# Feature group 1 of the last two token chunks by seven products, between groups 9 and 10; a weight split and a PSUM sum moved

## The chip, the cores and the metric

The kernel runs on one core of a Trainium2 chip. The metric is the device time of the program in microseconds (us), as the median of several runs. Engines are named as in the profile: PE (TensorE matmul), PEld (TensorE weight load), DVE (VectorE), ACT (ScalarE), POOL (GpSimd), SP (SyncE, which here only issues DMA transfers). L12 is line 12 of the kernel before. Differences of under about 0.2% of the time are not told from no change.

## The reference

One layer: a layer norm, a windowed dilated attention (S = 2048 tokens, D = 640, 32 heads of 20, 8 keys at a distance of 2), a bilinear feed-forward part with F = 1536 features, and a gate.

```python
xn = layernorm(x)
q, k, v = split_heads(xn @ wqkv)              # 32 heads of 20
idx = pos[:, None] - 2 * arange(8)            # 8 keys, dilation 2, masked below 0
attn = softmax(where(mask, q . k[idx] * scale, -1e9))
s = (attn . v[idx]) @ wo
h = (xn @ w_gate) * (xn @ w_up)               # 2048 x 1536
return x + s * silu(h @ w_down)
```

All is fp32.

## The kernel before, in words

*Products.* TensorE works on fp32r operands. Each fp32 operand is split into a high part (a copy by ACT, L114) and a low part (the difference, by POOL in L115 or by DVE), and a product is the sum of three: high by high, high by low, low by high (`ALL3`, L117; in `mm3` and in `group` the low part of the weights comes in the last third of the matmuls).

*Tiling of gate and up.* The tokens lie in four chunks of 512, the features in twelve groups f of 128 columns of gate and 128 of up. `gate_up(f, ch)` does group f for one chunk directly: 15 matmuls of 128x512 for gate, 15 for up (L124). `group(f, c0, second)` (L1253) does a pair of chunks (c0 and c0 + 1) and gate and up together by a seven-product scheme (Strassen's, in Winograd's form): 54 matmuls (L1292) in the order j = 0, 5, 2, 1, 4, 3, 6 into three PSUM banks, "g", "q" and "u". Between products ACT copies a bank to SBUF (`hold`, L1261, after the first, third, fourth and fifth product), DVE adds (`gate_b` L1264, `gate_a` L1274) and multiplies (`up_a` L1277), and `up_b` (L1267) and `h_b` (L1270) run on DVE for chunks 2 and 3, on POOL for chunks 0 and 1. A finished part of h goes to memory by SP (`store_h`, L1250). A bank is free for the next product when its hold is done.

*The weights of a group.* `load_wf(f)` brings the raw weights (640 KB, SP, L180). POOL makes five sums of their parts (S1, S2, S3, d5, S4; `w_add`, L1238), and they are split in four pieces by `w_split`: G (the tile "pk", read by the group's first product) and S, R, U (tiles "s"). Each split is an ACT copy, then a POOL difference. There are two "wraw" buffers for raw weights and for sums, so a load also waits until POOL has read the raw weights before it. The table `two_places` says after which product of which half of the group before each step is issued: the load after the first product of the first half, the sums from there to the second product of the second half, the splits in the second half.

*Order of the program.* Groups 0 and 1 are done early by `gate_up` on all four chunks, between the layer norm and the products of q, k and v (`qkv`). Groups 2 to 10 follow, each as two half-groups: chunks 2 and 3 (`group(f, 2)`), then chunks 0 and 1 (`group(f, 0, 1)`). Group 11 and the product with w_down come last. In the early part POOL also makes the sums of the tokens of chunks 0 and 1 that the seven products need (`early_sums`), and `early_high(k)` (L616, L617) makes their high and low parts, which SP stores for group 2 and later. `split_wq(1)` splits the weights of the next q, k, v products, on POOL for the low parts.

*The attention* is a generator that `advance(budget)` moves on by a sum of costs: products and reductions on DVE (L542, L549, L508), additions on POOL (L514), stores of the result by SP (L590). Each half-group gives it 54 x 0.184 units, each `qkv` after the start 1.9, each half (gate or up) of a `gate_up` there 3.25. What is left of it is flushed in group 10.

*The last loop* runs over products m of h with w_down (L866): `sum_h` (L813 and on) and `lo_h` (L829) on DVE prepare later products, `gather(m)` reads out PSUM on DVE (L882, L886, L889) or ACT, which frees the bank.

Every engine and every DMA queue works through its own list in the order of issue and waits on semaphores, so an instruction that waits holds up all behind it on its engine.

Of the kernel before, what the change touches and what calls it, by code (L numbers as in the profile page):

```python
# [12 lines left out]
F32R = mybir.dt.float32r  # L13
# [6 lines left out]
P = 128  # L20
# [9 lines left out]
TPC = CH // P  # L30
# [12 lines left out]
NP = NT // 2  # L43
PAIRS = range(0, W, 2)
PACE = 1.0
VEC = 2
EARLY = 1
GROUP_RATE = 0.184

# [7 lines left out]
def kernel(  # L57
# [70 lines left out]
    def slot(shape, dt=F32R):  # L128
        return st(shape, "s", SLOTS, dt)
# [48 lines left out]
    def load_wf(f):  # L178
        wf_raw[f] = slot([P, KD, 2, P], F32) if f == 0 else st([P, KD, 2, P], "wraw", 2)
        nc.sync.dma_start(wf_raw[f], wgu[f])  # L180
# [430 lines left out]
    def early_high(k):  # L611

        r0, r1, a, b = early_t[:4]
        for n, (j, y) in enumerate((("T1", a), ("T2", b), ("T3", r0), ("T4", r1))):
            hi = early_t[4 + n].bitcast(F32R)
            nc.gpsimd.tensor_copy(hi, y)  # L616
# [497 lines left out]
    gate_up(0, 2)  # L1114
    trans_q(15)
    low_parts()
    early_high(1)
    for a in range(2):
        nc.sync.dma_start(e_scr[2 + a], xT[3][a][:, 0:2, :].bitcast(F32))
    made.add(0)  # L1120
# [1 line left out]
    for i in range(TPC, NE):  # L1122
        qkv(0, 1, i)
        advance(PACE * 1.9)
    split_wq(1, nc.gpsimd)
    gate_up(1, 2)
    gate_up(0, 3)
    gate_up(1, 3)

    f0, f1 = KF - 2, KF - 1  # L1130
    F_TWO = 2
    tt, tw, steps = {0: [], 2: []}, {}, []
    T_UNIT = {(j, a, k): divmod(n, 3) for n, (j, a, k) in
              enumerate((j, a, k) for k in range(2) for j in ("T1", "T2", "T3") for a in range(2))}
# [66 lines left out]
    w_sum = {}  # L1201

    def two(f):
        return F_TWO <= f < f1

    def w_unit(f, name, k=0):

        t, n = W_UNIT[name]
        if t == "U" and two(f):
            t, n = "R", n + 1  # L1210
        if t not in tw:
            tw[t] = st([P, 2, KD, P], "pk", 1, F32R) if t == "G" and f >= F_TWO else slot([P, 2, W_ROWS[t], P])
        return [tw[t][:, i, n + k] for i in range(2)]

    def w_split(f, *names):
# [13 lines left out]
    def w_add(f, *names):  # L1229

        if f not in w_sum:
            w_sum[f] = st([P, 9, P], "wraw", 2)
        r, t = wf_raw[f], w_sum[f]
        v = {"A11": r[:, 0:2, 0], "A12": r[:, 2:4, 0], "A21": r[:, 0:2, 1], "A22": r[:, 2:4, 1], "g5": r[:, 4, 0],
             "u5": r[:, 4, 1], "S1": t[:, 0:2], "S2": t[:, 2:4], "S3": t[:, 4:6], "S4": t[:, 6:8], "d5": t[:, 8]}
        for name in names:
            a, b = W_SUM[name]
            nc.gpsimd.tensor_tensor(v[name], v[a], v[b], op=ALU.add if name == "S1" else ALU.subtract)  # L1238
# [14 lines left out]
    def group(f, c0=0, second=0):  # L1253

        b = {"A": pt([P, CH], "g", 2), "C": pt([P, CH], "u", 2), "B": q_one}
        kept, later = {}, []
        eng = nc.vector if c0 and f >= VEC else nc.gpsimd

        def hold(j):
            kept[j] = st([P, CH], "gh", 5)  # L1260
            nc.scalar.activation(kept[j], b["ACACABA"[j]], AF.Copy)  # L1261

        def gate_b():
            nc.vector.tensor_add(kept[2], kept[2], b["C"])  # L1264

        def up_b():
            eng.tensor_add(kept[1], kept[1], kept[4])  # L1267

        def h_b():
            eng.tensor_mul(kept[2], kept[2], kept[1])  # L1270
            store_h(f, c0 + 1, kept[2])

        def gate_a():
            nc.vector.tensor_add(kept[0], kept[0], b["B"])  # L1274

        def up_a():
            nc.vector.tensor_mul(kept[0], kept[0], b["A"])  # L1277
            store_h(f, c0, kept[0])

        if not second:  # L1280
            if not two(f - 1):
                w_split(f, "U")
            w_sum.pop(f, None)
            wf_raw.pop(f)
        for n, j in enumerate((0, 5, 2, 1, 4, 3, 6)):
            y = b["ACACABA"[j]]
            runs = [(w_unit(f, H_IN[j], k)[i], x_in(W_IN[j], l, k, c0)) for i, l in ALL3 for k in range(2)]
            if j in FIVE:
                name, ch = FIVE[j]
                runs += [(w_unit(f, name)[i], xT[c0 + ch][l][:, KD - 1, :]) for i, l in ALL3]  # L1290
            for r, (w, x) in enumerate(runs):
                nc.tensor.matmul(y, w, x, start=j in (0, 1, 5) and r == 0, stop=r == len(runs) - 1,  # L1292
                                 skip_group_check=True)
            if j in (0, 1, 2, 4):
                hold(j)
            finish_piece()
            if (second, n) == (1, 6) and (second, n) in places:
                places.pop((second, n))(f)
            for act in later:
                act()  # L1300
            later = {5: [gate_a], 3: [gate_b, up_b]}.get(j, [])
            if j == 6:
                unfinished.extend([up_a, h_b])
            if (second, n) in places:
                places[second, n](f)
            if (f, second, n) in beside:
                beside[f, second, n]()
            if (second, n) == (0, 0) and f < f1 and f + 1 not in wf_raw:
                load_wf(f + 1)
            advance(PACE * len(runs) * (GROUP_RATE if two(f) else 0.184))  # L1310

    places = {}
# [89 lines left out]

    wo_keep = []
    def sums(*names):
        return lambda f: w_add(f + 1, *names)

    def splits(*names):
        return lambda f: w_split(f + 1, *names)

    two_places = {(0, 5): sums("S1"), (0, 6): sums("S2"), (1, 0): sums("S3"), (1, 1): sums("d5", "S4"),  # L1410
                  (1, 2): splits("G"), (1, 4): splits("S"), (1, 5): splits("R"), (1, 6): splits("U")}
# [8 lines left out]
            load_e(1, 0, 0)  # L1420
            load_e(1, 1, 1)

    for f in range(2, f1):
        places.clear()
        places.update(two_places)
        if f == F_TWO:
            for n in range(3):
                places[0, n] = lambda f, n=n: load_late(n)
        group(f, 2)
        group(f, 0, 1)  # L1430
    places.clear()
    beside.update({(f1, 0, 0): lambda: split_wo(1, nc.vector),
                   (f1, 0, 2): lambda: (turn_pair(0), load_pair(1)), (f1, 0, 4): lambda: (hi_pair(0, 0), lo_pair(0, 0)),
# [193 lines left out]
```

## Time and profile before

| | us |
|---|---|
| median of three runs | 738.06 (738.04 to 738.15) |
| the profiled execution, own time | 737.74 |
| its span, first to last instruction | 735.7 |
| PE busy | 729.2 |
| DVE busy | 629.1 |
| POOL busy | 449.4 |
| ACT busy | 301.0 |
| mean granted clock of TensorE | 0.999 |

A row of a timeline gives start, duration (both in us), engine, line, operation, output and inputs, the tile's shape and the count of instructions in it; in square brackets stands how long the engine had idled before it and what ended that. A duration of several instructions is that of the whole stretch. An SPq row is SP issuing a transfer, not the transfer. In the chain of work that ended last, each piece has start, duration, and engine and line.

### The profile page before, as it was taken

How to read it: one execution, taken by the hardware profiler on the slowest of the kernel's cores; microseconds unless marked ns; L12 is line 12 of the kernel's file. 1: busy time of each engine (PE TensorE's matmuls, PEld its weight loads, DVE VectorE, ACT ScalarE, POOL GpSimd, SP SyncE). 2: the span in 40 equal slices, each digit the busy share in tenths (PEclk: the TensorE clock that was granted, in tenths of full speed). 3: DMA queues.
4: the chain of work that ended last, by engine and by line, in shares of the span. 5: the costliest groups of instructions: out<-in, count | busy, mean ns of one | idle time of the engine just before them, and what ended most of it. 6: DMA issues, size and time to landing. Idle time of an engine off the chain costs nothing.

```text
span 735.7 us, 11056 instructions
## 1 busy us (share of the span) xinstructions
PE 729.2 (99%) x4030; PEld 666.0 (91%) x4030; DVE 629.1 (86%) x729; ACT 301.0 (41%) x561; POOL 449.4 (61%) x383
## 2 busy tenths in 40 slices
PE   9999999999999999999999999999999999999997
PEld 7989989988999998888888887888999999999997
DVE  7676998799796989899989999978899897777775
ACT  5668312323232333233323332334556664444442
POOL 6159919997778889797889969667644630000000
PEclk9999999999999999999999999999999999999999
DMA  8464589889766659461733542277768955555534
GB/s 325 169 204 164 214 291 302 245 257 257 183 192 174 217 194 349 123 198 58 220 92 96 180 143 73 64 229 192 215 201 244 313 221 193 193 193 194 194 108 143
DMA packets 106436, 143.78 MB, mean 195 GB/s; under 512 B 23080, under 2 KB 75556, under 8 KB 106382
## 3 DMA queue, kind: packets, MB, share of 16 engines
q1 hardware_dynamic: 88654, 121.13, 51.8%
q10 hardware_dynamic: 16000, 12.78, 5.4%
q0 software_dynamic: 1728, 9.18, 5.2%
q8 instruction: 31, 0.51, 0.3%
q14 instruction: 23, 0.19, 0.1%
HBM read 94.40 MB, written 55.67 MB: 204 GB/s over the span
## 4 chain that ended last, share of the span: by engine, by line
PE 94%; DVE 3%; issue 1%; POOL 1%; DMA 1%; SPq 0%; ACT 0%; POOLq 0%; DVEq 0%
PE g L1292 15%; PE q L434 11%; PE u L1292 10%; PE u L434 8%; PE g L434 8%; PE q L866 8%; PE u L866 5%; PE q L1292 5%; PE g L124 5%; PE u L124 5%; PE q L996 3%; PE e L866 3%; PE g L866 3%; PE u L996 2%; PE e L996 2%; PE e L434 1%
## 5 line engine op out<-in xcount | busy, mean ns | idle before, releaser
L514 POOL TENSOR_TENSOR o<-o,t 128x960 f32<-128x960 f32 (+1 forms) x66 | 132.8, 2012 | 9.4 <-DVE t L508 8.5
L508 DVE TENSOR_TENSOR t<-e,kv 128x960 f32<-128x960 f32 (+1 forms) x96 | 99.6, 1038 | 16.2 <-POOL o L514 16.2
L542 DVE TENSOR_TENSOR t<-q,kv 128x1920 f32<-128x1920 f32 (+1 forms) x48 | 92.5, 1927 | 3.2 <-DMA kv<-qkv_scr 3.1
L549 DVE TENSOR_REDUCE lg<-t 128x96 f32<-128x1920 f32 (+1 forms) x48 | 92.3, 1924 | 0.2
L434 PE MATMUL q<-s,xc 128*128 128x360 f32 (+1 forms) x450 | 82.9, 334 | 0.1
L1261 ACT ACTIVATE gh<-g 128x512 f32<-128x512 f32 x57 | 34.1, 598 | 112.8 <-PE g L1292 108.0
L115 POOL TENSOR_TENSOR s<-wraw,s 128x384 fp32r<-128x384 f32 (+6 forms) x57 | 68.4, 1214 | 17.9 <-ACT s L114 17.8
L434 PEld LDWEIGHTS q<-s,xc 128*128 128x128 f32 x450 | 74.9, 188 | 4.2 <-ACT xc L314 0.3
L434 PE MATMUL u<-s,xc 128*128 128x360 f32 (+1 forms) x360 | 65.8, 334 | 0.0
L434 PEld LDWEIGHTS u<-s,xc 128*128 128x128 f32 x360 | 60.3, 188 | 2.2
L434 PE MATMUL g<-s,xc 128*128 128x360 f32 (+1 forms) x330 | 61.5, 338 | 0.0
L434 PEld LDWEIGHTS g<-s,xc 128*128 128x128 f32 x330 | 55.7, 188 | 2.6
L1292 PE MATMUL g<-s,s 128*128 128x512 f32 x228 | 58.0, 390 | 0.0
L1292 PE MATMUL u<-xc,s 128*128 128x512 f32 x228 | 57.9, 389 | 0.0
L866 PE MATMUL q<-xc,s 128*128 128x320 f32 x342 | 55.6, 310 | 0.6 <-DVE s L886 0.6
L866 PEld LDWEIGHTS q<-xc,s 128*128 128x128 f32 x342 | 51.5, 188 | 0.8 <-ACT s L847 0.8
L1292 PEld LDWEIGHTS g<-s,s 128*128 128x128 f32 x228 | 42.7, 188 | 9.2 <-ACT gh L1261 0.4
L1292 PEld LDWEIGHTS u<-xc,s 128*128 128x128 f32 x228 | 42.8, 188 | 8.9
L114 ACT ACTIVATE s<-wraw 128x384 fp32r<-128x384 f32 (+6 forms) x58 | 32.6, 581 | 30.3 <-PE g L1292 10.2
L1292 PE MATMUL g<-xc,s 128*128 128x512 f32 x171 | 42.0, 390 | 0.3 <-ACT gh L1261 0.3
L1292 PE MATMUL q<-xc,pk 128*128 128x512 f32 x171 | 41.9, 389 | 0.0
L514 POOL TENSOR_TENSOR o<-t 128x960 f32<-128x960 f32 (+1 forms) x11 | 22.2, 2014 | 28.3 <-DVE t L508 24.9
(332 smaller groups left out, 1561.3 us busy)
## 6 DMA issues: line engine op xcount, KB each, us to landing
h_scr<-gh SPq DMA_DIRECT2D x48, 256.0 KB, 2.6
wraw<-in_wgu SPq DMA_DIRECT2D x11, 640.0 KB, 4.5
kv<-qkv_scr SPq DMA_DIRECT2D x14, 480.0 KB, 5.9
t<-h_scr SPq DMA_DIRECT2D x8, 768.0 KB, 6.2
qkv_scr<-s ACTq DMA_DIRECT2D x17, 360.0 KB, 3.9
kv<-qkv_scr SPq DMA_DIRECT2D x14, 367.5 KB, 6.8
s_scr<-gh SPq DMA_DIRECT2D x16, 320.0 KB, 3.8
gh<-s_scr SPq DMA_DIRECT2D x16, 320.0 KB, 3.9
```

The costliest lines, as they stand in the source:

```text
L114: nc.scalar.activation(hi, raw, AF.Copy)
L115: eng.tensor_sub(lo, raw, hi.bitcast(F32))
L124: nc.tensor.matmul(acc, a, b, start=first and n == 0, stop=last and n == len(runs) - 1)
L434: nc.tensor.matmul(p, xT[(r * NE + i) // TPC][a][:, k, t0:t0 + P], wq[m][b][k], start=n == 0, stop=n == len(runs) - 1, skip_group_check=ac ...
L508: nc.vector.tensor_mul(t.rearrange("p (n d) -> p n d", d=DH), e[:, :, w].unsqueeze(2).to_broadcast([P, NE * nh, DH]), v)
L514: return NE * c * cost, lambda: eng.tensor_add(y, z, t)
L542: nc.vector.tensor_mul(t, q, k)
L549: nc.vector.tensor_reduce(out=lg[:, :, j:j + 2].rearrange("p n a -> p a n"), in_=t.rearrange("p a (n d) -> p a n d", d=DH), op=ALU.add, ax ...
L866: nc.tensor.matmul(p, y[:, i, k], wd_part(name, k, l), start=new and r == 0, stop=r == len(runs) - 1, skip_group_check=True)
L996: nc.tensor.matmul(b, y, w, start=new and r == 0, stop=r == len(runs) - 1, skip_group_check=True)
L1261: nc.scalar.activation(kept[j], b["ACACABA"[j]], AF.Copy)
L1292: nc.tensor.matmul(y, w, x, start=j in (0, 1, 5) and r == 0, stop=r == len(runs) - 1, skip_group_check=True)
```

## The change

1. `gate_up(1, 2)` and `gate_up(1, 3)` go. Group 1 of chunks 2 and 3 is done by `group(1, 2)`, between groups 9 and 10. Its weights are loaded a second time. The half-group that follows for every other f, on chunks 0 and 1, isn't there, as these are done early. All that prepares group 10's weights is therefore issued in this one half-group (`one_places`): the load after the first product, the five sums after the third, the splits G, S, R and U after the fourth to the seventh.
2. `split_wq(1)` comes after the second of the four `qkv` products that follow the attention's start, instead of after the last, and `early_high(1)`, which stood ahead of them, comes directly behind it.
3. In the last loop, the step at m = 3 no longer issues `sum_h(8)` and `lo_h(7)`; they are issued at m = 4, behind that step's read-out of PSUM.

```diff
-    early_high(1)
...
     for i in range(TPC, NE):
         qkv(0, 1, i)
         advance(PACE * 1.9)
-    split_wq(1, nc.gpsimd)
-    gate_up(1, 2)
+        if i == TPC + 1:
+            split_wq(1, nc.gpsimd)
+            early_high(1)
     gate_up(0, 3)
-    gate_up(1, 3)
+    wf_raw.clear()
...
-    F_TWO = 2
+    ORDER_F = [2, 3, 4, 5, 6, 7, 8, 9, 1, f0, f1]
+    after_f = dict(zip(ORDER_F, ORDER_F[1:]))
...
             finish_piece()
-            if (second, n) == (1, 6) and (second, n) in places:
+            if n == 6 and (second, n) in places and (second or f == 1):
                 places.pop((second, n))(f)
...
-            if (second, n) == (0, 0) and f < f1 and f + 1 not in wf_raw:
-                load_wf(f + 1)
+            if (second, n) == (0, 0) and f < f1 and after_f[f] not in wf_raw:
+                load_wf(after_f[f])
             advance(PACE * len(runs) * (GROUP_RATE if two(f) else 0.184))
...
     two_places = {(0, 5): sums("S1"), (0, 6): sums("S2"), (1, 0): sums("S3"), (1, 1): sums("d5", "S4"),
                   (1, 2): splits("G"), (1, 4): splits("S"), (1, 5): splits("R"), (1, 6): splits("U")}
...
-    for f in range(2, f1):
+    one_places = {(0, 2): sums("S1", "S2", "S3", "d5", "S4"), (0, 3): splits("G"), (0, 4): splits("S"),
+                  (0, 5): splits("R"), (0, 6): splits("U")}
+    for f in ORDER_F[:-1]:
         places.clear()
-        places.update(two_places)
+        places.update(two_places if f > 1 else one_places)
...
         group(f, 2)
-        group(f, 0, 1)
+        if f > 1:
+            group(f, 0, 1)
...
+        elif m == 4:
+            sum_h(m + AHEAD)
+            lo_h(m + AHEAD - 1)
...
         after()
+        if m == 3:
+            continue
```

The other lines of the diff only bring `two`, `w_unit`, `sums` and `splits` in line with the new order of groups. In the rows below, line numbers of the changed kernel are lower by one for the code ahead of the group function.

POOL's list around the start of group 9 in the kernel before: the end of group 8 (three splits, L1267 and L1270 of its chunks 0 and 1, additions of the attention, L514), then the sums for group 10, behind its load into wraw_3979:

```order
L115 TENSOR_TENSOR s_2460<-wraw_3857,s_2460 128x768
L115 TENSOR_TENSOR s_2645<-wraw_3857,s_2645 128x384
L115 TENSOR_TENSOR s_2645<-wraw_3801,s_2645 128x384
L1267 TENSOR_TENSOR gh_3923<-gh_3923,gh_3933 128x512
L514 TENSOR_TENSOR o_3771<-o_3771,t_942 128x960
L1270 TENSOR_TENSOR gh_3909<-gh_3909,gh_3923 128x512
L514 TENSOR_TENSOR o_3771<-o_3771,t_942 128x960 x2
L1238 TENSOR_TENSOR wraw_4032<-wraw_3979 128x256
```

POOL's list around the start of group 1 in the changed kernel: the end of group 9, then the five sums and the splits for group 10, behind its load into wraw_4074:

```order
L114 TENSOR_TENSOR s_2546<-wraw_3893,s_2546 128x384
L1267 TENSOR_TENSOR gh_4013<-gh_4013,gh_4023 128x512
L513 TENSOR_TENSOR o_3790<-o_3790,t_926 128x960
L1270 TENSOR_TENSOR gh_3999<-gh_3999,gh_4013 128x512
L1238 TENSOR_TENSOR wraw_4099<-wraw_4074 128x256
L1238 TENSOR_TENSOR wraw_4099<-wraw_4099,wraw_4074 128x256
L1238 TENSOR_TENSOR wraw_4099<-wraw_4074 128x256
L1238 TENSOR_TENSOR wraw_4099<-wraw_4074 128x128
L1238 TENSOR_TENSOR wraw_4099<-wraw_4074,wraw_4099 128x256
L114 TENSOR_TENSOR pk_2497<-wraw_4074,pk_2497 128x640
L114 TENSOR_TENSOR s_2362<-wraw_4099,s_2362 128x768
```

The sums and the split of pk now stand in the half-group that also has the load. On SP, the load stands directly behind the two stores of group 9's h for chunks 0 and 1, as in before (the second of them stores what L1270 makes).

ACT's list in group 1 of the changed kernel, with its holds (L1261; gh_4125 is the fourth) and the high parts of group 10's weights (L113):

```order
L1261 ACTIVATE gh_4068<-g_4060 128x512
L570 ACTIVATE e_70<-lg_3813 128x384
L1261 ACTIVATE gh_4096<-g_4060 128x512
L1261 ACTIVATE gh_4115<-u_4061 128x512
L113 ACTIVATE pk_2497<-wraw_4074 128x640
L1261 ACTIVATE gh_4125<-g_4060 128x512
L113 ACTIVATE s_2362<-wraw_4099 128x768
```

In before the copy of pk stands between the second and the third hold of the half-group on chunks 0 and 1; here it stands between the third and the fourth of the half-group on chunks 2 and 3.

DVE's list in the last loop, at m = 3 and 4, before:

```order
L882 TENSOR_TENSOR s_5442<-u_5360,gh_5405 128x320
L813 TENSOR_TENSOR s_5447<-s_5330,wraw_5334 128x768
L829 TENSOR_TENSOR s_5444<-wraw_5328,s_5444 128x768
L886 TENSOR_TENSOR s_5468<-lg_5379,q_1_68 128x320
L815 TENSOR_TENSOR s_5447<-s_5447,wraw_5328 128x768
```

and changed:

```order
L881 TENSOR_TENSOR s_5455<-u_5373,gh_5418 128x320
L885 TENSOR_TENSOR s_5478<-lg_5392,q_1_68 128x320
L812 TENSOR_TENSOR s_5480<-s_5343,wraw_5347 128x768
L828 TENSOR_TENSOR s_5457<-wraw_5341,s_5457 128x768
L814 TENSOR_TENSOR s_5480<-s_5480,wraw_5341 128x768
```

The sum that reads PSUM (L886, now L885) has moved ahead of the two operations on h.

More of the change, by code (lines that the diff above doesn't have):

```diff
@@ L45 @@
 PACE = 1.0
-VEC = 2
 EARLY = 1
@@ L1203, in two @@
     def two(f):
-        return F_TWO <= f < f1
+        return f < f1
     def w_unit(f, name, k=0):
@@ L1211, in w_unit @@
         if t not in tw:
-            tw[t] = st([P, 2, KD, P], "pk", 1, F32R) if t == "G" and f >= F_TWO else slot([P, 2, W_ROWS[t], P])
+            tw[t] = st([P, 2, KD, P], "pk", 1, F32R) if t == "G" else slot([P, 2, W_ROWS[t], P])
         return [tw[t][:, i, n + k] for i in range(2)]
@@ L1256, in group @@
         kept, later = {}, []
-        eng = nc.vector if c0 and f >= VEC else nc.gpsimd
+        eng = nc.vector if c0 else nc.gpsimd
         def hold(j):
@@ L1280, in group @@
         if not second:
-            if not two(f - 1):
+            if f == ORDER_F[0]:
                 w_split(f, "U")
@@ L1404, in sums @@
     def sums(*names):
-        return lambda f: w_add(f + 1, *names)
+        return lambda f: w_add(after_f[f], *names)
     def splits(*names):
-        return lambda f: w_split(f + 1, *names)
+        return lambda f: w_split(after_f[f], *names)
     two_places = {(0, 5): sums("S1"), (0, 6): sums("S2"), (1, 0): sums("S3"), (1, 1): sums("d5", "S4"),
@@ L1421, in load_late @@
             load_e(1, 1, 1)
-    for f in range(2, f1):
+    one_places = {(0, 2): sums("S1", "S2", "S3", "d5", "S4"), (0, 3): splits("G"), (0, 4): splits("S"),
+                  (0, 5): splits("R"), (0, 6): splits("U")}
+    for f in ORDER_F[:-1]:
         places.clear()
-        places.update(two_places)
-        if f == F_TWO:
+        places.update(two_places if f > 1 else one_places)
+        if f == ORDER_F[0]:
             for n in range(3):
```

## The prediction

> **What bounds the kernel now.** I read the page's first lines, then the waits of TensorE, then the chain in order of time around the places that the diff touches.
>
> ```profile
> span 735.7 us, 11056 instructions
> PE 729.2 (99%) x4030; PEld 666.0 (91%) x4030; DVE 629.1 (86%) x729; ACT 301.0 (41%) x561; POOL 449.4 (61%) x383
> DVE  7676998799796989899989999978899897777775
> ```
>
> TensorE is busy for 99% of the span, so the time is the number of matmuls times their pitch plus the few waits. These are all the waits of TensorE (who waited, for whom, sum in us, times, longest):
>
> ```profile
> PE q L229 <- POOL lg masks.py:199: 1.4, 1, 1.4
> PE q L866 <- DVE s L886: 0.6, 1, 0.6
> PE g L1292 <- ACT gh L1261: 0.3, 1, 0.3
> ```
>
> A change can therefore save matmuls, remove up to 0.9 us of late waits, or make new waits. The profiled execution took 737.74 us, the median of the runs 738.06: I make the sum against 737.74 and add 0.3 at the end.
>
> **Part 1, the matmuls: -1.36 us.** The chain in order of time has group 1 of chunk 2 (from 84.76) and of chunk 3 (from 98.36) in pieces of 15 matmuls; a later half-group by seven products follows, as busy time of PE, PEld, DVE, ACT, POOL, then granted clock, DMA share and GB/s of a window:
>
> ```profile
> 84.76 3.40 PE g L124 x15
> 98.36 3.40 PE g L124 x15
> 101.76 3.40 PE u L124 x15
> 456.65:468.90 12.25, 12.25 (x56) 10.14 (x55) 12.11 (x12) 4.32 (x8) 9.80 (x9) 1.00 0.42 121
> ```
>
> 15 matmuls in 3.40 us are 0.2267 us each, so the 60 removed are 13.60 us. The 54 of the new half-group are 54 x 0.2267 = 12.24 us (the window of 456.65 spans just that). All of it lies on TensorE's path: 12.24 - 13.60 = -1.36 us.
>
> **Part 1, what the new half-group has to carry: +5.8 us.** Every other feature group has two half-groups, 24.5 us, in which the next group's weights are loaded, summed on POOL and split into high and low parts; `two_places` begins the sums in the first half and the splits only in the second. Group 1 has one half-group of 12.24 us, and `one_places` puts it all there. Call its start T. Before has a near twin: the first half of group 9 (T = 443.84), ahead of which POOL has the same list as in the new order: splits of the weights with the attention's additions between, then L1267, an addition, L1270, with the next load on SP behind the store of what L1270 made. POOL's and SP's rows there (start, us; SPq is a queue's issuing time):
>
> ```profile
> 445.26 3.81 POOL L115 TENSOR_TENSOR s<-wraw,s 128x768 fp32r<-128x768 f32 x3
> 449.04 1.29 POOL L1267 TENSOR_TENSOR gh<-gh,gh 128x512 f32<-128x512 f32 x1
> 450.30 2.25 POOL L514 TENSOR_TENSOR o<-o,t 128x960 f32<-128x960 f32 x1
> 452.51 1.28 POOL L1270 TENSOR_TENSOR gh<-gh,gh 128x512 f32<-128x512 f32 x1
> 454.27 0.46 SPq L180 DMA_DIRECT2D wraw<-in_wgu  x1
> 458.52 0.97 POOL L1238 TENSOR_TENSOR wraw<-wraw 128x256 f32<-128x256 f32 x1 [0.17 <-DMA wraw<-in_wgu]
> 459.57 0.74 POOL L1238 TENSOR_TENSOR wraw<-wraw,wraw 128x256 f32<-128x256 f32 x1
> 460.27 1.69 POOL L1238 TENSOR_TENSOR wraw<-wraw 128x256 f32<-128x256 f32 x2
> 461.92 0.74 POOL L1238 TENSOR_TENSOR wraw<-wraw,wraw 128x256 f32<-128x256 f32 x1
> 462.92 1.57 POOL L115 TENSOR_TENSOR pk<-wraw,pk 128x640 fp32r<-128x640 f32 x1 [0.26 <-ACT pk L114]
> ```
>
> *The load.* Here it is issued at T+10.43 and the weights are there at 458.52, T+14.7. In the other rows of that load, the earliest that stands at a group's start is the one of 276.89 below, in the group that began at 272.20: T+4.69, with no L1270 to wait for. The load for group 11 lands at 482.14 in the group that began at 468.90, T+13.2:
>
> ```profile
> 272.20 1.52 PE L1292 MATMUL g<-xc,pk 128*128 128x512 f32 x6
> 276.89 0.35 SPq L180 DMA_DIRECT2D wraw<-in_wgu  x1
> DMA to landing us min/median/max: 4.1/4.6/11.8
> 482.14 0.73 POOL L1238 TENSOR_TENSOR wraw<-wraw 128x256 f32<-128x256 f32 x1 [7.45 <-DMA wraw<-in_wgu]
> 484.44 2.16 POOL L1238 TENSOR_TENSOR wraw<-wraw 128x256 f32<-128x256 f32 x2
> 487.40 1.57 POOL L115 TENSOR_TENSOR pk<-wraw,pk 128x640 fp32r<-128x640 f32 x1
> ```
>
> Were POOL done at T with all but the last of the three splits (1.3), L1267, the addition and L1270, then 1.3 + 1.29 + 2.25 + 1.28 would bring L1270's end to T+6.1; ACT's copy ahead of that split and SP's issuing, 0.8 together, make it T+6.9. With 4.1 to land, the short end for this order is T+11.0; the long end is the twin's T+14.7. I take the landing L = T+13.0, nearer to the twin, because POOL's list is the twin's, less a little because the attention, from which the additions come, is spaced wider ahead of it.
>
> *First wait.* ACT has the high part of the first product's weights ahead of the fourth hold (L1261) of group 1:
>
> ```profile
> 453.83 0.60 ACT L1261 ACTIVATE gh<-g 128x512 f32<-128x512 f32 x1 [2.30 <-POOL gh L1270]
> 461.61 0.60 ACT L1261 ACTIVATE gh<-g 128x512 f32<-128x512 f32 x1 [2.80 <-PE g L1292]
> 462.11 0.73 ACT L114 ACTIVATE pk<-wraw 128x640 fp32r<-128x640 f32 x1
> ```
>
> In before that split stands in a second half, with its data long there. In the new order it waits for the landing, and the hold, 0.60, waits behind it; the seventh product needs the bank that this hold empties. It is due at T + 45 x 0.2267 = T+10.2 and starts at L + 0.73 + 0.60 = T+14.3: 4.1 us.
>
> *Second wait.* POOL's five sums and the low part of those weights took from 458.52 to 464.49 after the landing, 5.97 us. Group 10's fifth matmul reads that low part. It is due at T + 12.24 + 4 x 0.2267 = T+13.15, or T+17.3 behind the first wait; the low part is there at T+18.97: 1.7 us more. Both together are 5.97 + 13.0 - 13.15 = 5.8 us. The next low parts need POOL some 1.9 us each against 3.4 us of matmuls until they are read, so the chain ends there. POOL's row of 487.40 ends 6.8 us after its landing, with DVE at work beside it, 0.9 more: the ends of this term are 11.0 + 5.3 - 13.15 = 3.1 (five sums of 0.74 and the split of 1.57) and 14.7 + 6.8 - 13.15 = 8.4.
>
> *Other costs of part 1.* Group 1's weights are loaded a second time, 640 KB, during group 9, in whose second half DMA is 0.42 busy (window above): 0. The attention loses four early steps and gains those of the new half-group: 13.0 units of its budget against 54 x 0.184 = 9.9, so 3.1 more are left for the flush in group 10. They fall on DVE, whose tenths fall from 9 to 7 in the last quarter: 0, and 2 us at most if TensorE's holds there come to wait for it. The wait of 0.3 us on L1261 is the twin's, at 453.83; in the new order the wait above stands at that place instead: -0.3.
>
> **Part 2, the split of q, k, v ahead of the early low parts: 0.** POOL's split runs here while the removed matmuls did:
>
> ```profile
> 81.42 0.62 POOL L616 CAST kv<-kv 128x512 fp32r<-128x512 f32 x1
> 89.17 4.39 POOL L115 TENSOR_TENSOR s<-wraw,s 128x1080 fp32r<-128x1080 f32 x3
> ```
>
> It ended at 93.56 (89.17 + 4.39), and the next products of q, k, v began at 105.16. Without the 13.60 us they come at 91.56. Put ahead of the early low parts (L616 and L617, POOL's instructions from 81.42 to 89.17 here), the split starts near 81.4 and ends near 86, 5 us in time. Behind the old order it would have been 2 us late: the cost if the cover is gone. The early parts and their stores come some 4 us later, and with them, on SP, a load for the attention's next unit; TensorE waits for neither there: 0.
>
> **Part 3, the PSUM sum ahead of h's: -0.6.** DVE's rows, and the matmul that waits:
>
> ```profile
> 596.66 1.23 DVE L813 TENSOR_TENSOR s<-s,wraw 128x768 f32<-128x768 f32 x1
> 597.81 0.94 DVE L829 TENSOR_TENSOR s<-wraw,s 128x768 fp32r<-128x768 f32 x1
> 598.68 0.47 DVE L886 TENSOR_TENSOR s<-lg,q 128x320 f32<-128x320 f32 x1
> 599.30 0.97 PE L866 MATMUL q<-xc,s 128*128 128x320 f32 x5 [0.57 <-DVE s L886]
> ```
>
> L886 goes ahead of 1.23 + 0.94 us of sums, and the wait of 0.6 goes. The two sums come 0.5 us later, for a product later still: 0, and 0.5 if that has no slack.
>
> **Sum.** 737.74 - 1.36 + 5.8 - 0.3 - 0.6 = 741.3, and 0.3 for the median: 741.6 us.
>
> **A rule on the clock.** TensorE's granted clock in the first 3 us, where it worked 1.65 of 3 us after a wait of 1.4:
>
> ```profile
> 0.00:3.00 3.00, 1.65 (x3) 1.04 (x4) 0.06 (x1) 1.28 (x1) 2.33 (x11) 1.00 0.36 107
> ```
>
> It is 1.00 at once, and I charge no slowing to the new wait of 4.1 us; no gap of before is that long, so none tests it. The Trainium skill, "TensorE: Matmul & The Clock Gate", section "Part 1: The HAM clock gate", says that after an idle window of about 3.4 us the array runs at half clock until it has been busy for about as long; the row of the first 3 us doesn't agree. The rule's result is rival C.
>
> **Rivals.**
> A. *The load is early, faster.* If POOL were a whole addition or two ahead of the twin and the load were issued by T+2.8 (landing T+7.2), all waits would vanish: 738.06 - 2.3 = 735.8. What decides is the time at which POOL ends L1270. For it: the load at 276.89. Against: that one waits for no L1270, and even with its T+4.69 the low part comes 0.9 us late (4.69 + 4.1 + 5.3 - 13.15), 736.7. Chance 0.06.
> B. *The short end.* L = T+11.0 with undisturbed sums: 738.06 - 2.26 + 3.1 = 738.9, no difference that counts. For it: the two halves ahead hold less attention. Chance 0.13.
> C. *The clock falls during the first wait.* The 13 matmuls between the two waits then take up to 5.9 us instead of 2.95: from T+14.3 to T+20.2, past the low part at T+19.0, so 1.2 more, 742.8. Against: 1.00 in the first 3 us. Chance 0.06. The page's rule is this mechanism.
> D. *DVE runs later than in the twin.* Its window of group 9's second half is 12.11 us busy of 12.25, and the additions on POOL wait for it; a further addition of 2.25 ahead of L1270 gives L = T+15.3 and slower sums: 741.6 + 2.3 + 0.9 = 744.8. Chance 0.11.
>
> **How the numbers follow.** The forecast, a landing between T+11.6 and T+14.7, has 0.64. About 0.2% (1.5 us, 736.6 to 739.5) is what a measurement of this kernel can tell from no change. Slower: forecast, C and D, 0.81; same: B, 0.13; faster: A, 0.06. The range 739.0 to 744.2 takes in the long end of the wait with disturbed sums (741.6 + 2.6) and on the other side the edge of B; it leaves out A, half of B and most of D.
>
> **What would show it.** In the profile of the changed kernel: TensorE's waits name ACT gh L1261 with some 4 us and POOL's split of pk with some 2, both in the half-group between 9 and 10; the load ahead of group 10 is issued about T+8.5 behind the store of the last h; the wait on L886 is gone; L1292 has 54 matmuls more and L124 60 fewer; nothing waits for the q, k, v splits near 91. I am wrong if the load is issued before T+5, if the raw weights of group 10 are there when ACT comes to them, or if DVE's flush in group 10 becomes a new wait.

## The result, and the profile after

The changed kernel took 747.64 us (median of six executions, 745.96 to 756.11) against 738.05 us before: a ratio of 1.0151 with a 95% interval of 1.0103 to 1.0199, 9.6 us slower. The forecast was 741.6 us, with a range up to 744.2. The sign was right, and the wait that was to carry it stands where it was put; the size was not.

The profiled execution was the longest of the six, 756.11 us. First its head and the waits of TensorE:

```profile
span 754.1 us, 11079 instructions
PE g L1292 <- ACT gh L1261: 4.8, 1, 4.8
PE u L1292 <- POOL s L114: 2.2, 1, 2.2
PE q L433 <- ACT s L447: 2.1, 2, 1.5
PE g L1292 <- DMA s<-t_scr: 1.9, 1, 1.9
```

The first row is the forecast one. The wait on the PSUM sum (L886 before, L885 now) is gone. The other three rows are in the products of q, k, v and at the entrance of group 2, where I had forecast nothing. A second profile of the same kernel, an execution of 749.03 us, is nearer to the median (`again`, first of the runs below; its wait of 1.4 us at the start of the program, as before, is left out):

```profile
PE g L1292 <- ACT gh L1261: 4.7, 1, 4.7
PE q L433 <- ACT s L447: 1.4, 1, 1.4
PE g L1292 <- DMA s<-t_scr: 0.6, 1, 0.6
```

*The half-group between 9 and 10* began at T = 467.50 in the profile of 756.11 us. POOL, SP's queue, ACT and TensorE, and then TensorE's clock in the window behind the wait (busy time of PE, PEld, DVE, ACT, POOL, then granted clock, DMA share, GB/s):

```profile
473.58 1.29 POOL L1270 TENSOR_TENSOR gh<-gh,gh 128x512 f32<-128x512 f32 x1
476.33 0.88 SPq L179 DMA_DIRECT2D wraw<-in_wgu  x1
481.40 0.74 ACT L113 ACTIVATE pk<-wraw 128x640 fp32r<-128x640 f32 x1 [6.22 <-DMA wraw<-in_wgu]
482.04 0.58 ACT L1261 ACTIVATE gh<-g 128x512 f32<-128x512 f32 x1
482.67 4.21 PE L1292 MATMUL g<-xc,s 128*128 128x512 f32 x9 [4.81 <-ACT gh L1261]
485.17 1.56 POOL L114 TENSOR_TENSOR pk<-wraw,pk 128x640 fp32r<-128x640 f32 x1
482.70:488.20 5.50, 5.50 (x13) 4.34 (x14) 2.10 (x3) 1.89 (x3) 5.50 (x6) 0.50 0.00 0
```

L1270 ends at T+7.4, the load is issued at T+8.8 behind the stores of h and lands at T+13.9; ACT's split and the hold follow, and the seventh product starts at T+15.2. Then the granted clock is 0.50, and 13 matmuls take 5.50 us, 0.42 each, where they take 2.95 at full clock. POOL's low part is ready at 486.73, T+19.2, but at half clock TensorE reaches it only later, so the second wait of the sum is not seen: the slow matmuls cover it.

*The products of q, k, v.* Two rows of TensorE in the kernel before; then TensorE, SP's queue and ACT in the second profile of the changed kernel:

```profile
105.00 2.56 PE L434 MATMUL q<-s,xc 128*128 128x360 f32 x15
107.40 2.56 PE L434 MATMUL g<-s,xc 128*128 128x360 f32 x15
103.67 2.56 PE L433 MATMUL u<-s,xc 128*128 128x360 f32 x15
107.63 2.74 PE L433 MATMUL q<-s,xc 128*128 128x360 f32 x15 [1.40 <-ACT s L447]
110.21 2.63 PE L433 MATMUL g<-s,xc 128*128 128x360 f32 x15
112.68 2.63 PE L433 MATMUL u<-s,xc 128*128 128x360 f32 x15
99.61 0.97 SPq L147 DMA_DIRECT2D wraw<-in_wqkv  x2
106.62 0.60 ACT L113 ACTIVATE s<-wraw 128x480 fp32r<-128x480 f32 x1 [4.12 <-DMA wraw<-in_wqkv]
```

ACT stands from 102.5 to 106.6 at the split (L113) of weights that are still in flight, and the copy L447 that frees a bank for TensorE waits behind it. And there is a second cost that no wait shows: fifteen matmuls take 112.68 - 110.21 = 2.47 us behind the wait, 164.4 ns each in the mean of the stretch, where those ahead of it, as those at the same place in the kernel before, take 2.40 us, 160.0 ns. In this profile some 680 matmuls of 360 columns go at the slower pitch; 57 of them, ahead of 46 us, do so in before too. The others, between 108 and 263 us, cost some 625 x 4.4 ns = 2.8 us.

*The last loop.* DVE in the second profile: the sum that reads PSUM (L885) goes ahead, as the change says.

```profile
608.42 0.47 DVE L885 TENSOR_TENSOR s<-lg,q 128x320 f32<-128x320 f32 x1
608.81 0.94 DVE L812 TENSOR_TENSOR s<-s,wraw 128x768 f32<-128x768 f32 x1
```

The second profile against before, 749.03 - 737.74 = 11.3 us: matmuls -1.4, old waits gone -0.9, the wait near 106 1.4, the slower pitch 2.8, the wait for token sums 0.6, the wait in group 1 4.7, half clock behind it 2.6. That is 9.8; the rest, 1.5 us, is in gaps under 0.5 us, such as the restart behind each wait and 0.4 us behind the last matmul.

### The profile page after: what moved, and what is told of

Its sections match the earlier page's. It is cut to its first block, busy times and chain, and to the rows that moved or that the text cites. A ratio compares the mean times of both kernels' runs of the same rounds, so it can differ in the third digit from the quotient of the medians.

```text
span 754.1 us, 11079 instructions
## 1 busy us (share of the span) xinstructions
PE 736.2 (98%) x4024; PEld 670.5 (89%) x4024; DVE 626.5 (83%) x731; ACT 304.9 (40%) x568; POOL 456.0 (60%) x392
## 5 line engine op out<-in xcount | busy, mean ns | idle before, releaser
L1261 ACT ACTIVATE gh<-g 128x512 f32<-128x512 f32 x60 | 36.0, 599 | 122.0 <-PE g L1292 116.1
L114 POOL TENSOR_TENSOR s<-wraw,s 128x384 fp32r<-128x384 f32 (+6 forms) x60 | 71.1, 1201 | 20.4 <-ACT s L113 20.4
L1292 PE MATMUL u<-xc,s 128*128 128x512 f32 x240 | 61.3, 390 | 2.2 <-POOL s L114 2.2
L1292 PE MATMUL g<-s,s 128*128 128x512 f32 x240 | 61.5, 391 | 1.9 <-DMA s<-t_scr 1.9
L1292 PEld LDWEIGHTS u<-xc,s 128*128 128x128 f32 x240 | 45.3, 189 | 12.1 <-POOL s L114 2.7
L1292 PEld LDWEIGHTS g<-s,s 128*128 128x128 f32 x240 | 45.0, 188 | 11.6 <-DMA s<-t_scr 2.3
L1292 PE MATMUL g<-xc,s 128*128 128x512 f32 x180 | 46.1, 402 | 4.8 <-ACT gh L1261 4.8
L113 ACT ACTIVATE s<-wraw 128x384 fp32r<-128x384 f32 (+6 forms) x61 | 34.6, 584 | 37.4 <-PE g L1292 9.7
L1292 PEld LDWEIGHTS g<-xc,s 128*128 128x128 f32 x180 | 34.9, 195 | 12.6 <-ACT gh L1261 5.2
L1292 PE MATMUL q<-xc,pk 128*128 128x512 f32 x180 | 44.1, 389 | 0.0
```

Source lines behind the costliest of these rows:

```text
L113: nc.scalar.activation(hi, raw, AF.Copy)
L114: eng.tensor_sub(lo, raw, hi.bitcast(F32))
```

## The experiments

Theory 1: three losses that add up, the late weights of group 10 (with the half clock), the early transfers that the 60 matmuls had covered, and the slower pitch that their wait starts. Rivals stand at each run. All ratios are to the kernel before, run beside it.

**again**: the changed kernel as it is.

> The changed kernel once more, for a second profile. Theory 1 (three losses that add up): the same waits stand at the same places: about 1.5 us near 106 for ACT's copy behind a split that waits for weights, 2 to 4 us at group 2's entrance (272 and 284) for POOL's low parts and a load of token sums, 4.8 us at the fourth hold of group 1, with half clock behind the long ones. Theory 2 (only the wait in group 1 is always there, the waits at 106 to 284 belong to the one profiled execution, which took 756.1 us where the others took 746 to 750): the profile shows the 4.8 us and little else, and its time is near 747.

Measured: 750.88 us (749.03 to 754.38), ratio 1.0174 (1.0148 to 1.0201). Its profile is shown above. The wait near 106, the pitch and the 4.7 us are in both profiles; the 2.2 us on POOL and the waits of 0.3 and 0.6 near 239 and 247 are in the longer one alone. So theory 1 holds for the first three, and the longer execution has something on top (last part of this section).

**load_first**: group 10's raw weights go on SP's queue ahead of group 9's last stores.

```diff
+        if f == 9:
+            places[1, 6] = lambda f: (w_split(1, "U"), load_wf(f0))
```

> The changed kernel, with group 10's raw weights loaded ahead of the two stores of group 9's h on SP instead of behind them. Theory 1: the load is issued about T+3 (when POOL has made the last low part from the raw buffer it takes over), lands about T+8, ACT's split is done before the fourth hold is due at T+10.2, POOL's low part is ready about T+13, when it is due; the wait of 4.8 us and the half clock behind it (2.6 us) go, so 6.5 to 7.6 us faster than the changed kernel, 740 to 741. Rival (POOL's sums, not the load, set the end): the first wait goes but a second of 3 to 4 us takes its place at group 10's fifth matmul, 744.

Measured: 742.82 us (740.95 to 744.25), ratio 1.0058 (1.0040 to 1.0076). Group 1 begins at T = 460.87 here:

```profile
462.54 0.35 SPq L179 DMA_DIRECT2D wraw<-in_wgu  x1
468.17 0.73 POOL L1238 TENSOR_TENSOR wraw<-wraw 128x256 f32<-128x256 f32 x1
468.44 0.73 ACT L113 ACTIVATE pk<-wraw 128x640 fp32r<-128x640 f32 x1
469.29 0.60 ACT L1261 ACTIVATE gh<-g 128x512 f32<-128x512 f32 x1
471.07 2.20 PE L1292 MATMUL g<-xc,s 128*128 128x512 f32 x9
471.49 2.50 POOL L114 TENSOR_TENSOR pk<-wraw,pk 128x640 fp32r<-128x640 f32 x1
```

The load leaves at T+1.7, ACT finds the weights there, the seventh product starts at its due time and the low part is ready at T+13.1, when it is due at T+13.15. Neither the wait nor the half clock is left: 8.1 us below again, 4.8 below the first runs, with 7.3 in the profile's own rows (4.7 and 2.6). Profile against profile it is 5.1 (749.03 and 743.92), as two waits of 0.8 and 1.0 us stand in groups 10 and 11 that the changed kernel doesn't have. The load's place set the end, not POOL's sums.

**warm** and **warm2**: 21 more matmuls of 512 columns ahead of the seventh product, so that TensorE works where it would wait (warm2's edit; warm took its weights from the tile that the awaited split writes).

```diff
+            if f == 1 and n == 6:
+                for r in range(21):
+                    nc.tensor.matmul(q_two[:, :CH], xT[3][0][:, 0, :P], xT[3][0][:, 0, :], start=True, stop=True)
```

> The changed kernel with 21 matmuls of 512 columns (4.76 us, results unused) ahead of group 1's seventh product, so that TensorE works while it would wait for the fourth hold. If the half clock behind the wait comes from the idle time: the clock stays 1.00 and the 13 matmuls behind take 2.95 us instead of 5.5; the second wait of my sum (for POOL's low part) shows, about 1 us; net 1 to 2 us faster than the changed kernel. If the half clock comes from something else: the 13 matmuls take 5.5 us as before and the time is the same.

Measured: 755.07 us (751.55 to 756.89). The extra matmuls waited 4.2 us for that tile, so they came on top of the wait; nothing follows for the clock.

> The run warm once more with operands that nothing rewrites (both from the tokens), since its 21 matmuls read the tile that the awaited split writes and so waited too. If idle time makes the half clock: granted clock 1.00 at the wait, the 13 matmuls behind take about 3 us, and a wait of about 1 us for POOL's low part shows in group 10; 1 to 2 us below the changed kernel. If not: half clock as before.

Measured: one execution, 752.47 us, with the 2.1 us on POOL of the longer executions. TensorE around the place, and its clock:

```profile
474.62 4.93 PE L1293 MATMUL q<-xc 128*128 128x512 f32 x21
479.39 2.23 PE L1296 MATMUL g<-xc,s 128*128 128x512 f32 x9
481.46 1.07 PE L1296 MATMUL g<-xc,pk 128*128 128x512 f32 x4
483.45 0.73 PE L1296 MATMUL g<-xc,pk 128*128 128x512 f32 x2 [0.92 <-POOL pk L114]
475.00:481.00 6.00, 6.00 (x28) 4.84 (x27) 4.54 (x5) 1.43 (x3) 2.87 (x4) 1.00 0.43 136
```

The clock stays at 1.00, the nine matmuls take 2.07 us where they took 4.01, and the second wait of the forecast's sum, 0.9 us for POOL's low part, comes out. So idle time makes the half clock. The whole time of this one execution says nothing, since it holds other waits.

**cover**: load_first with the two direct products of group 1 put back (their results are then made again by the half-group). With them come their stores and the 13.0 units of the attention's budget.

```diff
+    gate_up(1, 2)
     gate_up(0, 3)
+    gate_up(1, 3)
     wf_raw.clear()
```

> As load_first, with the two direct products of group 1 (60 matmuls) put back where they were; group 1 is done a second time between groups 9 and 10. Only the early cover differs from load_first. Theory 1 (the 60 matmuls covered transfers): the wait near 106, the slower pitch of 360 columns and the wait for token sums in group 2 are gone, so the time rises by less than the 13.6 us of matmuls: by 13.6 - 1.5 - 2.8 - 1.2 = 8 us, to 750 to 752. Rival (the early losses come from part 2's new order or are fixed costs of the program): the waits stay, and the time rises by 13.6, to 756.

Measured: 749.21 us (748.92 to 749.61), ratio 1.0150 (1.0135 to 1.0165): 6.4 us above load_first for 13.6 us of matmuls. The waits of TensorE are all of two rows, and TensorE, SP and ACT near 106:

```profile
PE q L228 <- POOL lg masks.py:199: 1.3, 1, 1.3
PE g L1294 <- ACT gh L1263: 0.5, 2, 0.3
105.14 2.56 PE L433 MATMUL q<-s,xc 128*128 128x360 f32 x15
107.54 2.56 PE L433 MATMUL g<-s,xc 128*128 128x360 f32 x15
100.48 1.68 SPq L147 DMA_DIRECT2D wraw<-in_wqkv  x2
112.91 0.60 ACT L113 ACTIVATE s<-wraw 128x480 fp32r<-128x480 f32 x1
```

The load is issued at 100.5 us, within 1 us of the changed kernel's 99.6, but its split is due at 112.9 here and was due at 102.5 there. So the load's time doesn't follow TensorE, and the 13.6 us were its cover. The pitch is 160.0 ns from 59 us on. This run also shows load_first's half-group alone: it holds no wait over 0.3 us. Taking the early matmuls away therefore cost some 7 us (13.6 - 6.4) against the 13.6 that it saved. Profile against profile it is 7.9 (13.6 less 749.61 - 743.92), and load_first's rows hold 7.2 that cover's don't: waits of 1.5 near 106 and 1.1 for token sums in group 2, 2.8 of slower pitch, and the 0.8 and 1.0 in groups 10 and 11. A further 0.4 near 8 us lies ahead of all that differs.

**early_only**: neither the early products nor the half-group (group 0's h is stored in place of group 1's).

```diff
-    ORDER_F = [2, 3, 4, 5, 6, 7, 8, 9, 1, f0, f1]
+    ORDER_F = [2, 3, 4, 5, 6, 7, 8, 9, f0, f1]
```

> The changed kernel without group 1 of chunks 2 and 3 altogether: the 60 early matmuls are gone and the half-group between 9 and 10 too (group 0's h is stored in its place). That leaves what the early removal alone costs. If it costs nothing: 738.05 - 13.6 - 0.6 = 723.9. Theory 1 (the 13.6 us covered transfers and the attention's work): 5 to 10 us more, 729 to 734, with waits of TensorE at the products of q, k, v near 106 and at group 2's entrance. Theory 2: 724 to 725.

Measured: 745.01 us, three of ten executions at 738 (the fastest, 737.65, is the profiled one), the others from 743.8 to 747.04; all far above both. It isn't clean: without the half-group the attention lacks 13 units, not 3, and its flush in group 10 held TensorE up, with half clock behind it:

```profile
PE u L1295 <- ACT gh L1264: 7.4, 1, 7.4
```

What it does show again is the wait of 1.4 us near 106 and the slower pitch (some 680 matmuls). Why most executions are 7 us longer than the profiled one is open.

**split_later**: the split on which ACT stood comes three steps later, and, as the last part of these weights is loaded at step `BLOCK[1] + 1`, that load does too (step 8, not 5).

```diff
+        BLOCK = (6, 7, 9, 10, 12) if m == 1 else (3, 4, 6, 8, 10)
```

> The changed kernel with the split of the third set of q, k, v weights three steps later (the first piece at step 6, not 3), so that ACT no longer waits for that load ahead of a copy that TensorE needs. Theory 1a (the wait of 1.4 us near 106 also starts the slower pitch, 164.4 instead of 160.0 ns for each of some 680 matmuls of 360 columns up to group 2): both go, and the time is 1.5 + 2.8 = 4.3 us below that of the changed kernel. Rival (the pitch comes from where the weights lie or from the memory traffic, not from the wait): only 1.5 us go and the pitch stays 164 ns.

Measured: 747.79 us (746.59 to 748.90), ratio 1.0133 (1.0118 to 1.0148). The changed kernel's ratios are 1.0151 and 1.0174, so the gain is between 1.3 and 3.0 us, in spreads as wide, and not the 4.3 expected. The wait left 106 and came back 22 us later, where ACT stands at the last part of the same weights:

```profile
122.62 0.35 SPq L147 DMA_DIRECT2D wraw<-in_wqkv  x1
127.99 0.60 ACT L113 ACTIVATE s<-wraw 128x480 fp32r<-128x480 f32 x1 [3.23 <-DMA wraw<-in_wqkv]
PE q L433 <- ACT s L447: 1.0, 1, 1.0
```

This is the load that the edit itself delayed: it is issued at 122.62 us here and at 111.40 in again, and lands 5.3 us later. What the later split alone would give is therefore not shown. But the pitch answered: 160 ns up to 127 us, 164 from 129 on. It follows the wait, not the place.

**reset**: 8 matmuls of 512 columns among the products of q, k, v, 10 us behind the wait.

```diff
             qkv(m, r, i)
+            if (m, n) == (1, 9):
+                y = pt([P, CH], "q", 3)
+                for _ in range(8):
+                    nc.tensor.matmul(y, xT[3][0][:, 0, :P], xT[3][0][:, 0, :], start=True, stop=True)
```

> The changed kernel with 8 more matmuls of 512 columns (results unused) in the q, k, v products, some 20 us behind the wait near 106. Theory 1a (the slower pitch is a state of the weight loads' lead that a stretch of longer matmuls ends): 164 ns ahead of the eight, 160 ns behind them up to the next wait; 1.8 us for the eight against some 2.4 us saved. Rival (memory traffic or place): 164 ns on both sides.

Measured: one execution, 748.18 us. TensorE around the eight (L1376):

```profile
114.34 2.63 PE L433 MATMUL q<-s,xc 128*128 128x360 f32 x15
116.81 2.00 PE L1376 MATMUL g<-xc 128*128 128x512 f32 x8
118.65 2.56 PE L433 MATMUL u<-s,xc 128*128 128x360 f32 x15
121.24 2.74 PE L433 MATMUL q<-s,xc 128*128 128x360 f32 x15
```

Behind them 15 matmuls are in 2.56 us again, and the next, behind a gap of 0.2 us (121.24 against 121.05), in 2.74. So the slower pitch is a state that a gap starts and that these eight ended; memory traffic and place are out. Not every stretch of longer matmuls ends it: in again, 240 matmuls of 480 columns stand between 132 and 184 us, and the 360 columns behind them, with no gap, are slow at once:

```profile
181.83 2.76 PE L433 MATMUL g<-s,xc 128*128 128x480 f32 x12
184.43 2.63 PE L433 MATMUL u<-s,xc 128*128 128x360 f32 x15
```

**w_later**: load_first with the four copies of w_down's blocks later.

```diff
-    W_SUMS = ((1, 2), (1, 12), (2, 4), (2, 12), (3, 7))
+    W_SUMS = ((1, 8), (1, 15), (2, 4), (2, 12), (3, 7))
```

> As load_first, with the four copies of w_down's blocks in memory (960 KB each) issued six steps later, so that they don't run beside the load of the next q, k, v weights, which took 7 us to land there. Theory 1b (these copies make that load late, since the removed h store no longer holds SP's queue back): the wait near 106 goes or falls below 0.3 us, the pitch stays at 160 ns until the next wait; 1.5 to 4 us below load_first's 742.8. Rival (as in split_later, all transfers together are the limit there): another wait of about 1 us between 110 and 140 takes its place, and the time stays within 1 us of load_first.

Measured: 742.88 us (740.38 to 744.82), ratio 1.0062 (1.0039 to 1.0085), as load_first; the wait near 106 is still 1.2 us. The copies are not what makes that load late: theory 1b falls.

**old_order**: load_first with part 2 undone.

```diff
+    early_high(1)
...
-        if i == TPC + 1:
-            split_wq(1, nc.gpsimd)
-            early_high(1)
+    split_wq(1, nc.gpsimd)
     gate_up(0, 3)
```

> As load_first, with part 2 undone: the early low parts ahead of the q, k, v weights' split. My sum: the split ends near 94, the products need it at 91.6, so 2 us later than load_first. Theory 1 adds that this wait starts the slower pitch some 14 us earlier (about 0.3 us more): 744 to 746. Rival (part 2's order itself delays SP's loads, and undoing it helps): 740 to 742.

Measured: 748.51 us (742.05 to 750.11), ratio 1.0113 (1.0064 to 1.0163). The wait for the split is 0.5 us, near 93, and the slower pitch begins there; the wait near 106 is gone and one of 1.1 us stands near 187. The profiled execution (749.65) has a wait of 2.4 us on POOL at group 2 on top. The median is 5.7 us above load_first's, but the fastest execution is below it: with a spread of 8 us the run doesn't tell part 2's worth.

**sum_only**: the kernel before with part 3 alone.

> The kernel before with part 3 alone (the PSUM sum ahead of h's sums in the last loop). Mine: the wait of 0.6 us on that sum goes and nothing takes its place: 737.3 to 737.5. Rival (the two delayed sums become late for the next products): 737.9 to 738.5.

Measured: 737.47 us (736.80 to 737.95), ratio 0.9986 (0.9978 to 0.9995). The wait on L886 is gone and none takes its place in the last loop (a wait of 0.7 us near 6 us lies ahead of all that the edit touches). It is 0.8 us below the kernel before beside it (738.28), with an interval of 0.4 to 1.6; the forecast had 0.6. This is the fastest version here, though by less than the 0.2% that I set as a bound.

**both** and **pace**: more budget for the attention, to give back what it lost. In both, 0.388 for 0.38 units per head in the products of q, k, v, with load_first and split_later; in pace, 0.1873 for 0.184 per matmul of a group, with copy_apart below.

> The changed kernel with the load ahead of the stores (as in load_first), the later split (as in split_later), and 2% more budget for the attention in the q, k, v products (3.3 units, what the change lost). Theory 1: load_first's 742.8 less 4.3 for the split and its pitch, less 1 to 2 for waits in group 10 and 11 that hang on the attention's backlog: 736.5 to 738.5, about the kernel before; it beats the kernel with part 3 alone (737.5) only at the low end.

Measured: 750.49 us (749.24 to 751.05), ratio 1.0168 (1.0152 to 1.0183).

> As copy_apart, with 1.8% more budget for the attention per matmul of a feature group (3.0 units over 17 half-groups, what the change lost). Theory: the waits of TensorE in groups 10 and 11 (0.8 us for a hold near 493, 1.0 for the product on a bank near 514) go: 1.5 to 2 us below copy_apart. Rival (POOL's and DVE's lists are full there, so the same work only comes to wait elsewhere): within 0.5 us of copy_apart or above.

Measured: 751.23 us (749.96 to 754.30), ratio 1.0181 (1.0159 to 1.0203). Waits of TensorE in the profile of both, then of pace:

```profile
PE g L1292 <- ACT pk L113: 2.5, 1, 2.5
PE g L1292 <- POOL pk L114: 1.9, 1, 1.9
...
PE g L1292 <- ACT gh L1261: 3.8, 2, 3.4
PE g L1292 <- POOL pk L114: 2.7, 1, 2.7
```

With 2% more attention per step both lie some 8 us above load_first and copy_apart; in both, split_later's delayed load may have its part in that. TensorE's new waits are for splits and holds that come late, which fits lists of POOL and DVE that were full already; the lists were not followed further. The waits of some 1 us in groups 10 and 11 that pace was to remove did go, at that price.

**copy_apart** and **after_apart**: the spread. Two executions of the same kernel part near 209 us; POOL's first addition of an attention unit there, in the profile of 756.11 us and in that of 749.03:

```profile
218.81 2.26 POOL L513 TENSOR_TENSOR o<-t 128x960 f32<-128x960 f32 x1 [8.77 <-DMA o_scr<-o]
212.73 2.27 POOL L513 TENSOR_TENSOR o<-t 128x960 f32<-128x960 f32 x1 [3.08 <-DVE t L507]
```

In the first it waits for the store of the unit before, which took 12.2 us to land (5.8 in the other). In both executions SP issued it 1.2 us ahead of a copy of 960 KB on POOL's queue. The attention is 6 us late from there, and POOL 2 us late at group 2. The profiles of old_order and warm2 show the same wait of 8.6 and 8.7 us, and are long too. The edit in both runs (on load_first, and on the changed kernel):

```diff
-    W_SUMS = ((1, 2), (1, 12), (2, 4), (2, 12), (3, 7))
+    W_SUMS = ((1, 2), (1, 12), (2, 4), (2, 12), (3, 2))
```

> As load_first, with the last of the copies and sums of w_down's blocks (960 KB on POOL's queue, near 207 us) issued five steps earlier. Theory 3 (in slow executions the store of an attention unit lands 12 us after its issue, not 6, beside this copy; POOL's next addition waits 8.7 us for it, and POOL is late at group 2): no slow executions, all between 740 and 742.5, and no wait of over 5 us of POOL's L513 for that store. Rival (the spread has another cause): medians and spread as load_first, 741 to 744.3.

Measured: 742.54 us (742.22 to 743.41), ratio 1.0058 (1.0044 to 1.0072): load_first's time, with a spread of 1.2 instead of 3.3 us.

> The changed kernel with only the last copy of w_down's blocks issued five steps earlier. Theory 3: its executions, 746 to 756 so far, come to lie within 2 us, near 748 to 750; no wait of POOL's L513 of over 5 us near 209 to 219. Rival (another cause): they still spread over 5 us or more, some above 752.

Measured: 748.58 us, four executions from 746.88 to 751.40 (a fifth took 2,411 us and is left out), ratio 1.0146 (1.0120 to 1.0172). None above 752, but 4.5 us of spread. So the late store is where the two profiles part, but that the copy is the cause, and the only one, is not shown: POOL also waits for such a store for 7.7 us near 180 in pace and for 6.8 in early_only.

## Why the prediction was right and wrong

*Right.* The half-group between 9 and 10 is too short for group 10's weights, by the chain as told: landing at T+13.9 (forecast 13.0, a choice between 11.0 and the 14.7 of the twin in group 9), ACT's split and the hold behind it, first wait 4.8 (4.1), low part at T+19.2 (18.97). load_first shows that this chain alone cost 7 us or so. Part 3 gave 0.8 (0.6). The 54 matmuls take their 12.24 us.

*The second wait and the clock.* The sum had 1.7 us for the wait on the low part and nothing for the clock. Measured: no second wait, but 2.6 us of half clock; 7.4 for the whole term against 5.8. That is rival C, to which I gave 0.06. My argument against it was the clock of 1.00 in the first 3 us, where the longest wait is 1.4 us, and that was no test: behind the waits of 1.0 to 1.5 us near 106 the clock stays 1.00 here too, and behind those of 4.2 to 7.4 it fell every time. The Trainium skill, "TensorE: Matmul & The Clock Gate", section "Part 1: The HAM clock gate", has half clock behind an idle window of some 3.4 us and a gap of 427 ns between cold matmuls of 512 columns; this trace agrees, with 0.50 and 13 matmuls in 5.50 us. On the length of the wait the runs decide: here the clock also fell behind waits of 1.9 to 2.7 us (last section).

*The step that failed.* "Part 1, the matmuls: -1.36 us. All of it lies on TensorE's path" counted what the 60 matmuls took and not what they covered, and the entry for the q, k, v weights looked at one load only, the set that is split at that place, and found it 5 us in time. The next set, issued at 99.6 us and landing at 106.6, was the one in need of cover. Its price in the second profile is 1.4 us of waiting, 2.8 us of slower pitch and 0.6 us for the token sums in group 2 (0 to 1.9 in the other profiles), 4.8 us where the sum had 0; cover, in which these matmuls were put back with their stores and their budget, puts it at some 7 us. 741.6 + 4.8 + 1.6 is 748.0, against medians of 747.64 and 750.88.

*The attention's lost budget* was to cost 0, and 2 at most. In load_first's profile two waits of 0.8 and 1.0 us stand in groups 10 and 11, and in cover, which gives the budget back and has no wait over 0.3 us behind the start, they are gone: 1.8 us, near the upper end. They are gone in pace too, but that run has waits of 3.4 and 2.7 us ahead of them. The changed kernel's own profiles don't have them either; that its wait in group 1 lets DVE and POOL catch up would explain it, but was not tried.

*Part 2* had no term but a doubt: that without it the split would come 2 us late. old_order has 0.5 us of that. Its own delay of SP's list, which I put at 0, can't be read off these runs.

*What stays open.* Why the store near 206 us sometimes takes 12 us, and with it the spread of the changed kernel; and why 2% more attention cost 8 us. Of cover's 7.9 us, 5.4 are the pitch and the waits up to group 2, and 1.8 the waits in groups 10 and 11; that the latter are the attention's rests on the budget that cover gives back, not on a run that changes it alone.

## What to carry to other kernels

Work that is taken away from a saturated engine is also cover that is taken away: list every transfer whose landing the removed stretch stood over, the ones issued during it and used behind it above all, before booking the saving. A step that was spread over two stages by a table can't be put into one of them without asking where its load stands in its queue; moving that one load ahead of two stores gave back 4.8 to 8.1 us of a loss of 9.6 to 12.6. And a wait costs more than its length when it is long enough for the clock to fall.

## What the runs showed of the hardware

A gap of 0.2 to 1.5 us in a run of matmuls of 360 columns was followed by a slower steady pitch, 164.4 instead of 160.0 ns, which showed in all such matmuls up to 263 us; 8 matmuls of 512 columns ended it (reset), and the next small gap started it again. The 240 matmuls of 480 columns in between take 216.7 ns each in either state and did not end it, but for the run both, where a gap stands among them and the 360 columns behind went at 160.0 ns. In all ten kernels with a wait near 106 us the slower pitch follows it; in the three without any wait from 60 to 260 us (before, sum_only, cover) it isn't there in that time. It costs 2.7% of such a stretch and shows in no list of waits.

The clock fell behind waits of some 2 us too, but not always. In the profile of 756.11 us it was 0.60 behind a wait of 1.9 us, and in warm2 0.74 behind one of 2.1 us:

```profile
286.10:289.60 3.50, 3.50 (x10) 2.77 (x11) 3.43 (x6) 1.23 (x2) 2.94 (x4) 0.60 1.10 379
275.00:280.00 5.00, 5.00 (x18) 3.98 (x17) 4.23 (x5) 0.60 (x1) 4.99 (x6) 0.74 1.02 346
```

while the matmuls behind the wait of 2.2 us near 272 in the first of these profiles went at full pitch. Over all profiles, by the pitch of the matmuls behind: none of the waits from 0.9 to 1.5 us was followed by half clock, three of five from 1.8 to 2.3 us were (1.86, 1.89 and 2.13, but not 1.83 and 2.24), and all eleven from 2.4 us on.
